# Float32 products for batches 0 and 1, and feed-forward weights taken unit by unit of both products

## The chip, the cores and the metric

The kernel runs on one core of one Trainium2 chip. Time is device microseconds of one execution. Before the change it is 1036.37 us, the median of three runs (1036.07 to 1036.69). The engines are TensorE (PE; its weight loads are shown as PEld), VectorE (DVE), ScalarE (ACT), GpSimd (POOL) and SyncE (SP), whose queue issues nearly all DMAs, the transposing ones too.

## The reference

Eight batches of eight heads, 576 tokens, 64 values a head. An attention with 32 memory slots is followed by a Fourier mix over tokens and channels and a feed-forward block of 512 to 2048 to 512:

```python
a = softmax(phi, over tokens)                  # 576 x 32 for each head
k_m, v_m = a.T @ k, a.T @ v                    # 32 x 64 each
x = softmax(q @ k_m.T / 8, over slots) @ v_m
u = x + real(fft(fft(x, tokens), channels))
ch = relu(layernorm(u) @ w_ch1) @ w_ch2
out = u + ch
```

All arrays are float32 and the result must be near float32.

## The kernel before

**Numbers.** To be near float32, most products are made of float16 halves: an operand is scaled, rounded to float16 (the high half), and the rest is rounded again (the low half); three products (high by high, low by high, high by low) are added in PSUM. Making halves takes a pass of ACT and a pass of DVE, or of ACT twice and POOL.

**Weights.** They arrive as 64-bit words (the host hands them over unchanged), 1 MB for each of NW = 8 units of `w1` and 8 of `w2`. `load_stage` (L710) brings a unit into a staging area; `to_f32` (L717) makes float32 of it: an Abs on ACT (L724), a shift and two combining passes on DVE (L726, L727, L737; for the units in `LP` the last is L732 on DVE and L735 on POOL), a sum of squares on ACT (L746) and a small product on PE (L220), from which `norm_scale` (L228, L236, L239) takes a power of two. `split_w1` (L752) and `prepare_w2` (L788) then write the float16 halves over the same memory.

**A batch** is the generator `background` (L810), which yields between steps. `pooling_weights` (L288) transposes phi on PE, takes the softmax over tokens, makes halves in `elt` and brings them back to token order in `et` by a transposing DMA (L319, helper L244). `pair_memory` (L323), for each of four pairs of heads, finds scales (L331 to L343), makes halves of k and v (L345 to L352) and multiplies by `et` in 30 float16 products of 64 columns (tile `pm`). `pair_scores` (L391) makes halves of q (L397, L398), 18 products (`psc`), the softmax over slots (L412 to L427) and sums and differences of tokens (L434 to L451). `values` (L465), `spectrum` (L500), `mix_m` (L547), `mix_x` (L532) and `add_mix` (L579) then make the rows of `u`: a batch has three groups of rows, t = 0, 1 and 2; group 2 is half a tile and shares its tile with the next batch's.

**Feed-forward.** The rows go in 18 chunks of two tiles of 128. `norm_chunk` (L612) normalises a chunk; for chunk 0 it transposes on PE and keeps float32, for the others it makes halves and uses a transposing DMA (`unring<-ud`). Chunk 0 goes through `ffn1_direct` (L634) and `ffn2_direct` (L649) in float32, the others through `ffn1` (L662, tile `ph`) and `ffn2` (L686, tile `po`), with relu and halves on ACT and DVE (L680, L681).

**Order.** The code's order is: batch 0 to its first two tiles; chunk 0 normalised; a loop over the 8 units of `w1`, each converted, used for chunk 0 and split, with the rest of batch 0 inside (`MB`, `M1`); a loop over the 8 units of `w2` that loads and converts them, with `norm_chunk(1)` inside (`N1`); then `advance(0)` (L887), which takes batch 1 as far as the ring of eight `u` tiles lets it (L890); then the main loop (L922), which for chunk 0 runs `ffn2_direct`, and beside it `ffn1` of the chunk after, and one step of a batch for each unit. Chunk 2 needs rows of batch 1. From this a planner, which simulates the engines, makes each engine's queue: it may take an instruction earlier than the code has it when its operands and memory are free in the simulation, and `tc.issue_after` forbids that for single instructions. On the chip each queue runs in its order, so an instruction that waits holds all behind it on its engine.

**Memory.** Staging areas of the weights (`W1_STAGE`, `W2_STAGE`, L705) lie in parts of `w2s` that are not yet in use and in the three areas of `stg`; `stg` is also where odd pairs of heads land (L277) and, from batch 1 on, where halves of k, v and q lie (L188 to L197).

Of the kernel before, what the change touches and what calls it, by code (L numbers as in the profile page):

```python
# [40 lines left out]
MB = 5  # L41
M1 = 2
N1 = 4
D2 = 8
# [10 lines left out]
W1_STAGE = [14, "0", "1", "2", 14, "0", "1", "2"]  # L55
W2_STAGE = [10, 14, "0", "1", 14, "0", "1", "0"]
# [75 lines left out]
def kernel(  # L132
# [50 lines left out]
    nc.gpsimd.memset(elt[:, :, S:], 0.0)  # L183
# [4 lines left out]
    def halves_area(b):  # L188

        if b == 0:  # L190
            v = hring[:, NHS:].rearrange("p a l b c -> p (a l b c)")
            t = w1t[:, NW].rearrange("p l k c -> p (l k c)")
        else:
            v = stg[:, 2]
            t = v[:, 4 * NST * P :]
        v = v[:, : 4 * NST * P].rearrange("p (l t w c) -> p l t w c", l=2, t=NST, w=2)
        return v, t[:, : 2 * NQ].rearrange("p (l c) -> p l c", l=2)  # L197
# [74 lines left out]
    def load_pair(b, g):  # L272
        r = rawt
        if b == 0 and g > 0:
            r = w2s.rearrange("p a l c -> p (a l c)").bitcast(F32)[:, RKQ * (g - 1) : RKQ * g]
        elif g % 2 == 1:
            r = stg[:, 0].bitcast(F32)  # L277
        nc.sync.dma_start(out=r[:, :KV], in_=raw[b, g, :, :KV])
        marks["q"] = nc.sync.dma_start(out=r[:, KV:], in_=raw[b, g, :, KVP:])
        return r  # L280
# [7 lines left out]
    def pooling_weights(b):  # L288
# [24 lines left out]
        for g in range(2):  # L313
            r = su[:, 2 + g : 3 + g]
            nc.scalar.activation(elt[:, 0, :S], pht[:, g], AF.Copy, scale=r)
# [7 lines left out]
    def pair_memory(b, g, r, vmf, ivs):  # L323
# [4 lines left out]
        kvs, _ = halves_area(b)  # L328
        am = tiny("am", 3, 1)
        for w in range(2):  # L330
            nc.scalar.activation(  # L331
                kvs[:, 0, :, w, :].bitcast(BF16), kv[:, :, w, :], AF.Square, accum_out=am[:, 1 + w : 2 + w]
            )
        nc.scalar.activation(
            kvs[:, 1, 0:3].rearrange("p t w c -> p (t w c)").bitcast(BF16), q, AF.Square, accum_out=am[:, 0:1]
# [8 lines left out]
        for w in range(2):  # L344
            nc.scalar.activation(kvs[:, 0, :, w, :], kv[:, :, w, :], AF.Copy, scale=sc[:, 1 + w : 2 + w])  # L345
            if w in KP:
                nc.scalar.activation(kv[:, :, w, :], kv[:, :, w, :], AF.Copy, scale=sc[:, 1 + w : 2 + w])  # L347
                nc.gpsimd.tensor_tensor(  # L348
                    out=kvs[:, 1, :, w, :], in0=kv[:, :, w, :], in1=kvs[:, 0, :, w, :], op=ALU.subtract
                )  # L350
            else:
                nc.vector.scalar_tensor_tensor(  # L352
                    out=kvs[:, 1, :, w, :],
                    in0=kv[:, :, w, :],
                    scalar=sc[:, 1 + w : 2 + w],
                    in1=kvs[:, 0, :, w, :],
# [3 lines left out]
        for w in range(2):  # L360
            i = 0
            for ka, kb in ((0, 0), (1, 0), (0, 1)):
                for t in range(NST):
                    mm(
                        pm[:, w * 64 : w * 64 + 64],
                        lhsT=kvs[:, ka, t, w, :],
# [24 lines left out]
    def pair_scores(b, g, q, sc, km, es, aeo):  # L391
# [4 lines left out]
        _, qs = halves_area(b)  # L396
        nc.scalar.activation(qs[:, 0], q, AF.Copy, scale=sc[:, 0:1])  # L397
        nc.vector.scalar_tensor_tensor(  # L398
            out=qs[:, 1], in0=q, scalar=sc[:, 0:1], in1=qs[:, 0], op0=ALU.mult, op1=ALU.subtract
        )  # L400
        for t in range(6):
            for i, (qa, ka) in enumerate(((0, 0), (1, 0), (0, 1))):
                mm(
                    psc[:, t * 64 : t * 64 + 64],
                    lhsT=qs[:, qa, t * P : (t + 1) * P],
# [21 lines left out]
        nc.gpsimd.tensor_tensor(out=a, in0=a, in1=sm.unsqueeze(2).to_broadcast([P, 12, M]), op=ALU.mult)  # L427
# [8 lines left out]
        for i, op in ((12, ALU.add), (16, ALU.subtract)):  # L436
            nc.gpsimd.tensor_tensor(out=a2[:, i : i + 4], in0=a[:, 0:4], in1=a[:, 4:8], op=op)  # L437
# [8 lines left out]
        nc.scalar.copy(out=aeo[:, 0, :, gs], in_=eov)  # L446
# [4 lines left out]
        nc.vector.scalar_tensor_tensor(  # L451
# [10 lines left out]
    def pair_transpose(b, g, ahl, attnT):  # L462
        transpose(attnT[:, g], ahl.rearrange("p t c -> p (t c)"), False, f"attnT_{b}_{g}")

    def values(b, vmf, ivs):  # L465
# [4 lines left out]
        nc.vector.tensor_reduce(out=isg, in_=ivs, axis=AX.X, op=ALU.max)  # L470
        nc.vector.reciprocal(out=sg, in_=isg)
# [8 lines left out]
        transpose(vbdt, vms.rearrange("p l g u c -> p (l g u c)"), False, f"vbd_{b}")  # L480
        vt = vts[min(b, 1)]
# [163 lines left out]

    def h_f32(j):
        return hring[:, j].rearrange("p l f c -> p (l f c)").bitcast(F32).rearrange("p (f t c) -> p f t c", f=UB, t=CH)
# [14 lines left out]
    def ffn1(c, unT, j, hs):  # L662
# [15 lines left out]
        h = hring[:, (c * NW + j) % NHS]  # L678
# [26 lines left out]
    def stage_area(i):  # L705
        if isinstance(i, str):
            return [stg[:, int(i)].bitcast(I32)]
        return [w2s[:, i : i + 2 * UB].rearrange("p a l c -> p (a l c)").bitcast(I32)]
# [8 lines left out]
    def to_f32(stages, dst, key):  # L717
# [28 lines left out]
        marks["sq" + key] = nc.scalar.activation(stages[0].bitcast(BF16)[:, :UW], dst, AF.Square, accum_out=sq[:, 0:1])  # L746
# [18 lines left out]
    def prepare_w1(j):  # L765

        t = w1_f32(j)
        if j not in parts_w1:
            parts_w1[j] = load_stage(w1[j], stage_area(W1_STAGE[j]))
        top = to_f32(parts_w1[j], t, f"1_{j}")  # L770
        s = s1[:, j : j + 1]
        norm_scale(s, is1[:, j : j + 1], top, 1, 9, f"w1_{j}")
# [4 lines left out]
    def stage_w2(j):  # L777
        top = to_f32(load_stage(w2[j], stage_area(W2_STAGE[j])), w2_f32(j), f"2_{j}")
# [31 lines left out]
    def background():  # L810
# [3 lines left out]
        for b in range(B):  # L814
# [6 lines left out]
            yield nt, 0  # L821
            for step in range(NG + 2):
                if step < NG and b == 0:
                    mem[step] = pair_memory(b, step, first[step], vmf, ivs)
                    yield nt, 0
                elif step < NG:
                    r = load_pair(b, step)
                if step >= 2:
# [9 lines left out]
            at = spectrum(b, aeo)  # L838
            full = slice(0, P)
# [164 lines left out]
```

## Time and profile before

| | |
|---|---|
| median of three runs | 1036.37 us |
| the profiled execution | 1033.89 us |
| its span, first to last instruction | 1032.1 us |
| mean granted TensorE clock | 0.977 |
| PE busy | 934.4 us, 91% |
| DVE busy | 592.0 us, 57% |
| ACT busy | 496.4 us, 48% |
| POOL busy | 240.8 us, 23% |

A busy PE is a PE with a product in flight; the ends of products are modelled, so the starts tell the rate. A row of the table by stage gives the stretch, its length, then for each engine the busy time and in brackets the number of instructions, then the granted clock of TensorE, the mean busy share of the DMA engines and GB/s. A row of the groups gives line, engine, operation, output and inputs, shapes and count, then busy time in all and the mean of one in ns, then the idle time ahead of them. A row of the chain of waits gives the start, the duration and what was running or waited for; the chain is followed backwards from the last instruction, so what is not in it could have been later.

### The profile page before, as it was taken

How to read it: one execution, taken by the hardware profiler on the slowest of the kernel's cores; microseconds unless marked ns; L12 is line 12 of the kernel's file. 1: busy time of each engine (PE TensorE's matmuls, PEld its weight loads, DVE VectorE, ACT ScalarE, POOL GpSimd, SP SyncE). 2: the span in 40 equal slices, each digit the busy share in tenths (PEclk: the TensorE clock that was granted, in tenths of full speed). 3: DMA queues.
4: the chain of work that ended last, by engine and by line, in shares of the span. 5: the costliest groups of instructions: out<-in, count | busy, mean ns of one | idle time of the engine just before them, and what ended most of it. 6: DMA issues, size and time to landing. Idle time of an engine off the chain costs nothing.

```text
span 1032.1 us, 19009 instructions
## 1 busy us (share of the span) xinstructions
PE 934.4 (91%) x7736; PEld 662.1 (64%) x7736; DVE 592.0 (57%) x1331; ACT 496.4 (48%) x986; POOL 240.8 (23%) x268
## 2 busy tenths in 40 slices
PE   1245999954999999999999999999999999999998
PEld 0224767634777677777676777777776777766664
DVE  5885966775676676557752467656745575311111
ACT  6563857655663655466541346365534553411110
POOL 1142432432331232233211013132221231300000
PEclk9996999976999999999999999999999999999999
DMA  9930454332531553154401173136312521201000
GB/s 357 308 71 19 195 180 113 74 105 44 138 95 38 101 121 87 39 113 119 85 28 41 18 163 96 38 55 162 92 48 37 120 15 38 41 21 35 8 22 20
DMA packets 124662, 90.30 MB, mean 87 GB/s; under 512 B 109344, under 2 KB 109344, under 8 KB 122272
## 3 DMA queue, kind: packets, MB, share of 16 engines
q1 hardware_dynamic: 124576, 89.10, 33.9%
q8 instruction: 60, 0.98, 0.4%
q14 instruction: 26, 0.21, 0.1%
HBM read 58.15 MB, written 9.44 MB: 65 GB/s over the span
## 4 chain that ended last, share of the span: by engine, by line
PE 85%; DVE 5%; DMA 3%; ACT 2%; POOL 2%; issue 1%; SPq 1%; DVEq 0%; POOLq 0%
PE ph L261 34%; PE po L690 33%; PE pp_t L261 3%; PE pm L261 3%; PE ph L641 3%; PE po L654 3%; PE psc L261 1%; PE px_t L261 1%; DMA w2s<-in_raw 1%; PE pa L514 1%; PE pv L487 1%; DMA et<-elt 1%; DMA unring<-ud 1%; DVE uring L583 1%; POOL ud L628 1%
## 5 line engine op out<-in xcount | busy, mean ns | idle before, releaser
L261 PE MATMUL ph<-unring,w1t 128*128 128x256 f16 x3264 | 392.1, 273 | 12.4 <-DMA unring<-ud 12.4
L690 PE MATMUL po<-w2s,hring 128*128 128x512 f16 x1632 | 378.0, 379 | 0.0
L261 PEld LDWEIGHTS <-w1t 128*128 128x128 f16 x3336 | 320.8, 99 | 79.5 <-DVE scratch L603 12.5
L690 PEld LDWEIGHTS <-hring 128*128 128x128 f16 x1632 | 157.6, 98 | 158.8
L681 DVE SCALAR_TENSOR_TENSOR hring<-ph,hring 128x512 f16<-128x512 f32 x136 | 93.3, 686 | 165.5 <-ACT hring L680 165.1
L680 ACT ACTIVATE hring<-ph 128x512 f16<-128x512 f32 x136 | 80.2, 590 | 168.9 <-PE ph L261 168.7
L427 POOL TENSOR_TENSOR aring<-aring,scratch 128x384 f32<-128x384 f32 x30 | 25.0, 834 | 178.5 <-DVE scratch L426 163.8
L261 PEld LDWEIGHTS <-stg 128*128 128x128 f16 x1344 | 54.1, 99 | 15.7 <-issue 3.6
L607 POOL TENSOR_TENSOR scratch<-scratch,small 128x1 f32<-128x1 f32 x36 | 21.9, 612 | 153.2 <-DVE scratch L606 143.1
L348 POOL TENSOR_TENSOR stg<-rawt,stg 128x640 f16<-128x640 f32 x14 | 20.5, 1461 | 135.2 <-ACT rawt L347 125.2
L628 POOL TENSOR_TENSOR ud<-un,ud 128x1024 f16<-128x1024 f32 x17 | 36.2, 2129 | 46.7 <-ACT ud L627 46.7
L261 PE MATMUL pp_t<-vh,at 128*128 128x255 f16 (+3 forms) x288 | 41.1, 291 | 1.7 <-ACT at L529 1.5
L261 PE MATMUL pm<-et,hring 128*128 128x64 f16 x120 | 8.2, 241 | 35.7 <-DMA et<-elt 18.6
L569 DVE SCALAR_TENSOR_TENSOR share<-pp_t,scratch,small 128x257 f32<-128x257 f32 (+1 forms) x48 | 21.1, 481 | 32.5 <-ACT small L566 32.3
L422 ACT ACTIVATE aring<-aring,scratch 128x384 f32<-128x384 f32 x30 | 18.2, 608 | 43.0 <-DVE aring L421 43.0
L261 PE MATMUL pm<-et,stg 128*128 128x64 f16 x840 | 34.9, 194 | 4.4 <-POOL stg L348 2.7
L446 ACT CAST aeo<-eo 128x384 f16<-128x384 f32 x30 | 15.3, 510 | 45.2 <-DVE eo L443 45.1
L261 PEld LDWEIGHTS <-at 128*128 128x128 f16 (+1 forms) x288 | 30.0, 109 | 8.2 <-ACT at L529 1.8
L583 DVE SCALAR_TENSOR_TENSOR uring<-px_t,scratch,share 128x256 f32<-128x256 f32 (+1 forms) x80 | 33.9, 476 | 0.2
L627 ACT CAST ud<-un 128x1024 f16<-128x1024 f32 x17 | 17.8, 1045 | 33.4 <-DVE un L608 25.1
L412 DVE TENSOR_REDUCE scratch<-psc 128x12 f32<-128x384 f32 x32 | 17.8, 555 | 27.9 <-PE psc L261 27.8
L437 POOL TENSOR_TENSOR aring<-aring 128x128 f32<-128x128 f32 x60 | 33.2, 574 | 2.3
(199 smaller groups left out, 1318.6 us busy)
## 6 DMA issues: line engine op xcount, KB each, us to landing
stg<-in_w SPq DMA_DIRECT2D x11, 1024.0 KB, 8.5
rawt<-in_raw SPq DMA_DIRECT2D x15, 640.0 KB, 4.5
out<-uring SPq DMA_DIRECT2D x36, 256.0 KB, 2.1
stg<-in_raw SPq DMA_DIRECT2D x14, 640.0 KB, 4.8
rawt<-in_raw SPq DMA_DIRECT2D x15, 384.0 KB, 3.3
stg<-in_raw SPq DMA_DIRECT2D x14, 384.0 KB, 3.1
phs<-in_raw SPq DMA_DIRECT2D x32, 160.0 KB, 3.9
w2s<-in_w SPq DMA_DIRECT2D x5, 1024.0 KB, 6.4
```

Source lines behind the costliest of these rows:

```text
L261: m = nc.tensor.matmul(out, lhsT=lhsT, rhs=rhs, start=start, stop=stop)
L427: nc.gpsimd.tensor_tensor(out=a, in0=a, in1=sm.unsqueeze(2).to_broadcast([P, 12, M]), op=ALU.mult)
L437: nc.gpsimd.tensor_tensor(out=a2[:, i : i + 4], in0=a[:, 0:4], in1=a[:, 4:8], op=op)
L569: nc.vector.scalar_tensor_tensor(out=tm[rows, w * NJ : (w + 1) * NJ], in0=pp[rows, :NJ], scalar=beta[rows], in1=qs[rows], op0=ALU.mult, op ...
L583: nc.vector.scalar_tensor_tensor(out=u[rows, hs], in0=px[rows, hs], scalar=igx[rows], in1=tm[rows, w * NJ + half : w * NJ + half + 256], o ...
L607: nc.gpsimd.tensor_tensor(out=rs, in0=rs, in1=half, op=ALU.pow)
L628: marks[f"ul{c}"] = nc.gpsimd.tensor_tensor(out=ud[:, 1], in0=un, in1=ud[:, 0], op=ALU.subtract)
L641: nc.tensor.matmul(ph, lhsT=w[:, k, f * P : (f + 1) * P], rhs=unTs[0][:, k], start=(k == 0), stop=(k == NK - 1))
L654: nc.tensor.matmul(po[t], lhsT=h[:, f, t], rhs=w[:, f], start=(j == 0 and f == 0), stop=(j == NW - 1 and f == UB - 1),)
L680: nc.scalar.activation(h[:, 0], phv, AF.Relu)
L681: nc.vector.scalar_tensor_tensor(out=h[:, 1], in0=phv, scalar=0.0, in1=h[:, 0], op0=ALU.max, op1=ALU.subtract)
L690: nc.tensor.matmul(po[t], lhsT=hs[j][:, lh, f * 2 + t], rhs=w2s[:, j * UB + f, lw, :], start=(j == 0 and f == 0 and i == 0), stop=(j == NW ...
```

## The change

- Batches 0 and 1 (`b < NX`) keep the pooling weights in float32 (`et32`, in the memory of `et`), transposed on PE; `pair_memory` makes ten float32 products of k and v as they come, and `pair_scores` six float32 products of q. The scales and halves of k, v, q and km are left out for these batches; `values` finds its scale from a sum of squares.
- For batch 0 the transposes of the attention weights and of the values are made on PE and copied by ACT, and three steps of `pair_scores` go from POOL to DVE.
- In batch 0 all four `pair_memory` come ahead of the scores in the code. The loads of its pairs are tied to one another in order and the weights' loads come behind them, three units of both products at once.
- One loop over the units: load, convert `w1`, `ffn1_direct`, convert `w2`, `ffn2_direct`, split `w1`, two steps of the batches. The conversions but the first of `w1` may not start ahead of chunk 0's normalisation (`GATE1`, `GATE2`: on DVE not ahead of the mark `un1`, L608; on ACT not ahead of `uh0`, L624).
- Staging areas: parts of `w1t`, of `w2s`, `stg` 1 and 2, and once the end of `hring` with two tiles of `uring`. Batch 1's pairs use `rawt` and `stg` 0. The sum of squares writes its unused output to `elt`.
- Chunk 0 is finished ahead of the main loop, which starts at chunk 1; four units of chunk 1's `ffn1` are in the code ahead of `norm_chunk(2)`.

```diff
+STEPS = 2
+NX = 2
+GATE1 = [[]] + [["un1", "uh0"]] * 7
+GATE2 = [["un1", "uh0"]] * 8
-W1_STAGE = [14, "0", "1", "2", 14, "0", "1", "2"]
-W2_STAGE = [10, 14, "0", "1", 14, "0", "1", "0"]
+W1_STAGE = ["w4", "w6", "s1", "w6", "s1", "s2", "s1", "x"]
+W2_STAGE = ["b10", "b14", "s2", "b10", "b14", "x", "s2", "s1"]
...
-    nc.gpsimd.memset(elt[:, :, S:], 0.0)
+    nc.gpsimd.memset(et.rearrange("p g l t c -> p (g l t c)"), 0.0)
...
@@ in load_pair @@
+        for part, src in ((r[:, :KV], raw[b, g, :, :KV]), (r[:, KV:], raw[b, g, :, KVP:])):
+            with tc.issue_after(marks["q"].ins) if b == 0 and "q" in marks else nullcontext():
+                marks["q"] = nc.sync.dma_start(out=part, in_=src)
...
@@ in pooling_weights @@
+            if b < NX:
+                nc.scalar.activation(pht[:, g], pht[:, g], AF.Copy, scale=r)
+                pt = psg.tile([P, 512], F32, tag="g", name=f"pt_e{b}_{g}")
+                for t in range(4):
+                    nc.tensor.transpose(pt[:, t * P : (t + 1) * P], pht[:, g, t * P : (t + 1) * P], identf)
+                nc.vector.tensor_copy(out=et32[:, g, :4], in_=pt.rearrange("p (t c) -> p t c", c=P))
+                half_t = pl[0 : S - 4 * P, (2 + g) * P : (3 + g) * P]
+                nc.tensor.transpose(half_t, pht[:, g, 4 * P :], identf)
+                nc.scalar.copy(out=et32[0 : S - 4 * P, g, 4], in_=half_t)
+                continue
...
@@ in pair_memory @@
+        if b < NX:
+            pm = psg.tile([P, 512], F32, tag="g", name=f"pm_{n}")
+            mm = groups()
+            for w in range(2):
+                for t in range(NST):
+                    mm(
+                        pm[:, w * 64 : w * 64 + 64],
+                        lhsT=kv[:, t, w, :],
+                        rhs=et32[:, g // 2, t, 64 * (g % 2) : 64 * (g % 2) + 64],
+                        start=(t == 0),
+                        stop=(t == NST - 1),
+                    )
+            kmf = share[:, g * 64 : g * 64 + 64] if b == 0 else tiny("kmf", 64, 2)
+            nc.vector.tensor_tensor(out=kmf, in0=pm[:, 0:64], in1=mk[:, 0:64], op=ALU.mult)
+            nc.vector.tensor_tensor(
+                out=vmf[:, g],
+                in0=pm[:, 64:128].unsqueeze(1).to_broadcast([P, 2, 64]),
+                in1=mk[:, 0:64].unsqueeze(1).to_broadcast([P, 2, 64]),
+                op=ALU.mult,
+            )
+            return q, None, kmf, 1.0 / 8.0
...
@@ in pair_scores @@
+        if b < NX:
+            for t in range(6):
+                mm(psc[:, t * 64 : t * 64 + 64], lhsT=q[:, t * P : (t + 1) * P], rhs=km, start=True, stop=True)
...
+        eng = nc.gpsimd if b else nc.vector
+        eng.tensor_tensor(out=a, in0=a, in1=sm.unsqueeze(2).to_broadcast([P, 12, M]), op=ALU.mult)
...
-            nc.gpsimd.tensor_tensor(out=a2[:, i : i + 4], in0=a[:, 0:4], in1=a[:, 4:8], op=op)
+            eng.tensor_tensor(out=a2[:, i : i + 4], in0=a[:, 0:4], in1=a[:, 4:8], op=op)
...
-        transpose(attnT[:, g], ahl.rearrange("p t c -> p (t c)"), False, f"attnT_{b}_{g}")
+        transpose(attnT[:, g], ahl.rearrange("p t c -> p (t c)"), b == 0, f"attnT_{b}_{g}")
...
@@ in stage_area @@
+        if name[0] == "s":
+            return [stg[:, i].bitcast(I32)]
+        if name[0] == "w":
+            return [w1t[:, i : i + 2].rearrange("p a l k c -> p (a l k c)").bitcast(I32)]
+        if name[0] == "b":
+            return [w2s[:, i : i + 2 * UB].rearrange("p a l c -> p (a l c)").bitcast(I32)]
+        return [
+            hring[:, 6:8].rearrange("p a l f c -> p (a l f c)").bitcast(I32),
+            uring[:, 5:7].rearrange("p a c -> p (a c)").bitcast(I32),
+        ]
...
+    for j in range(3):
+        load_weights(j)
...
     for j in range(NW):
-        prepare_w1(j)
-        if j == M1:
-            while made < MB:
-                made, room = next(bg)
+        if j not in parts_w1:
+            load_weights(j)
+        after(GATE1[j], prepare_w1, j)
         ffn1_direct(j)
+        after(GATE2[j], stage_w2, j)
+        ffn2_direct(j, po)
         split_w1(j)
-    for j in range(NW):
-        after([f"2_{j - D2}"] if j >= D2 else gate, stage_w2, j)
-        if j == N1:
+        advance(0, steps=STEPS)
+        if made >= 2 * CH and 1 not in unTs:
             unTs[1] = norm_chunk(1)
+    nc.gpsimd.memset(elt[:, :, S:], 0.0)
     scale_w2()
+    finish(0, po)
     vts.append(load_vt())
+    prepare_w2()
...
-    advance(0)
-    for n in range(n_steps):
+    run_ffn1(NW + 4)
+    advance(CH, CH * 3)
+    unTs[2] = norm_chunk(2)
+    for n in range(NW, n_steps):
...
-        run_ffn1(n + NHS)
+        run_ffn1(n + 4 if n + 4 <= 2 * NW else n + NHS)
```

`load_weights(n)` issues the loads of unit n of `w1` and of `w2`, each into its staging area and each behind the one before.

More of the change, by code (lines that the diff above doesn't have):

```diff
@@ L186 @@
     hring = const.tile([P, NW, 2, 4, P], F16, name="hring")
[L188 to L197, printed above, removed]
+    nk = 2 * NST * P
+    kvs = [stg[:, 2, i * nk : (i + 1) * nk].rearrange("p (t w c) -> p t w c", t=NST, w=2) for i in range(2)]
+    qs = [stg[:, 2, 2 * nk + i * NQ : 2 * nk + (i + 1) * NQ] for i in range(2)]
+    et32 = et.rearrange("p g l t c -> p (g l t c)").bitcast(F32).rearrange("p (g t c) -> p g t c", g=2, t=NST)
     nc.gpsimd.memset(half, -0.5)
@@ L445, in pair_scores @@
         eov = eo.rearrange("p e t c -> p (e t) c")
-        nc.scalar.copy(out=aeo[:, 0, :, gs], in_=eov)
+        marks[f"a{b}_{g}"] = nc.scalar.copy(out=aeo[:, 0, :, gs], in_=eov)
         av4 = aeo.rearrange("p l (e t) c -> p l e t c", e=2)
@@ L703, in finish, with stage_area @@
             nc.sync.dma_start(out=out[idx], in_=u)
[L705 to L708, printed above, removed]
+    def stage_area(name):
+        i = int(name[1:] or 0)
+        if name[0] == "s":
[8 more added lines that the diff above has]
+        ]
     def load_stage(src, stages):
@@ L821, in background @@
             yield nt, 0
+            if b == 0:
+                for g in range(NG):
+                    mem[g] = pair_memory(b, g, first[g], vmf, ivs)
             for step in range(NG + 2):
[L823 to L826, printed above, removed]
+                if step < NG and b > 0:
                     r = load_pair(b, step)
-                if step >= 2:
+                if step >= 2 and b > 0:
                     pair_transpose(b, step - 2, ahl.pop(step - 2), attnT)
@@ L870, with load_weights @@
     marks["load"] = marks["q"]
-    parts_w1 = {0: load_stage(w1[0], stage_area(W1_STAGE[0]))}
     with tc.issue_after(marks["load"].ins):
         vts = [load_vt()]
-        nc.sync.dma_start(out=ct, in_=ct_d)
+        marks["load"] = nc.sync.dma_start(out=ct, in_=ct_d)
+    parts_w1, parts_w2 = {}, {}
+    def load_weights(n):
+        for parts, w, stages in ((parts_w1, w1, W1_STAGE), (parts_w2, w2, W2_STAGE)):
+            parts[n] = load_stage(w[n], stage_area(stages[n]))
+    for j in range(3):
+        load_weights(j)
     bg = background()
```

80 lines of the change are left out of this document (38 added, 42 removed).

## The prediction

> **What bounds the kernel now.** I read the page's head first, then the table by stage, then the chain of waits.
>
> ```profile
> span 1032.1 us, 19009 instructions
> PE 934.4 (91%) x7736; PEld 662.1 (64%) x7736; DVE 592.0 (57%) x1331; ACT 496.4 (48%) x986; POOL 240.8 (23%) x268
> PE   1245999954999999999999999999999999999998
> ```
>
> PE is busy for 934 of 1032 us, and the slices say where the other 98 us lie: in the first four slices and in the ninth to eleventh. The stages are cut at the events that end them.
>
> ```profile
> 0.00:100.48 100.48, 32.01 (x303) 24.92 (x304) 71.79 (x147) 53.48 (x98) 24.35 (x39) 0.92 0.57 191
> 100.48:160.00 59.52, 59.52 (x259) 41.90 (x258) 46.39 (x101) 42.80 (x69) 21.68 (x10) 0.99 0.48 168
> 160.00:209.30 49.30, 49.30 (x426) 33.64 (x425) 33.66 (x61) 35.00 (x64) 17.47 (x16) 1.00 0.47 109
> 209.30:255.40 46.10, 21.15 (x199) 15.73 (x198) 31.27 (x84) 25.39 (x57) 11.21 (x14) 0.70 0.24 60
> 500.00:900.00 400.00, 400.00 (x3449) 284.51 (x3447) 228.84 (x531) 188.55 (x393) 93.05 (x107) 1.00 0.31 68
> ```
>
> The front, up to chunk 0's first float32 product at 100.5, leaves PE idle for 100.5 - 32.0 = 68.5 us. The direct products (to 160) and chunk 1 (to 209.3) fill PE. Then PE waits 25 us, 46.1 - 21.2, for the rows of batch 1. From 255.4 on PE is full, and the change leaves that part's work alone. So **the time is set by when chunk 2 starts: 255.4**, and each microsecond by which it starts earlier is one off the end.
>
> ```profile
> 6.93 15.02 DMA w2s<-in_raw
> 22.04 9.89 DMA et<-elt
> 251.01 4.27 DMA unring<-ud
> 255.41 6.11 PE ph L261 x41
> ```
>
> In the front the chain stands first on a load of batch 0's pairs, 15 us, behind four loads of weights, and then on a transposing DMA, 9.9 us. After that it is mostly DVE.
>
> **The front.** What DVE does there for the weights is one row, its instructions on `w1t` up to 100.48; behind it the same row for L352 and for L398, to 255.4, and groups of what else goes:
>
> ```profile
> 0.00:100.48 100.48, 30.92 (x28) 0.92 0.57 191
> 0.00:255.40 255.40, 7.92 (x9) 0.91 0.47 146
> 0.00:255.40 255.40, 12.15 (x9) 0.91 0.47 146
> L384 DVE TENSOR_TENSOR scratch<-scratch 128x64 f16<-128x64 f32 x8 | 2.6, 328 | 4.1 <-ACT scratch L383 4.1
> L316 DVE SCALAR_TENSOR_TENSOR elt<-phs,scratch,elt 128x576 f16<-128x576 f32 x5 | 4.1, 819 | 5.1 <-ACT elt L315 5.0
> L236 DVE TENSOR_SCALAR scratch<-scratch 128x3 f32<-128x3 f32 x9 | 2.0, 220 | 0.1
> L298 DVE TENSOR_REDUCE scratch<-pf 128x1 f32<-128x512 f32 x6 | 4.1, 684 | 6.4 <-PE pf L297 6.4
> L421 DVE TENSOR_TENSOR aring<-psc,scratch 128x384 f32<-128x384 f32 x6 | 3.3, 550 | 0.0
> ```
>
> All of the `w1` conversion (24 instructions) is now inside the front, with four halves of q: 30.9 of DVE's 71.8 us. For batch 0 there also go four L352 (7.92 / 9 = 0.88 each, 3.5 us), two L316 (1.6), four L384 (1.3) and some 25 instructions on scales, at most 0.22 each, say 5.5. That leaves 71.8 - 30.9 - 3.5 - 1.6 - 1.3 - 5.5 = 29. Added: two copies of `et32` like L298 (1.4), and per pair what comes over from POOL, one like L421 (0.55) and two like the L439 below (0.29), together 4.5. The first `w1` unit's conversion stays, 0.7 + 1.2 + 1.2 and three scales, 3.6. Sum 38.5 us.
>
> ```profile
> 0.00:25.00 25.00, 3.19 (x12) 2.36 (x12) 13.77 (x24) 14.93 (x27) 3.91 (x14) 1.00 0.93 354
> 50.00:75.00 25.00, 10.45 (x118) 7.28 (x119) 21.72 (x50) 15.40 (x29) 14.01 (x17) 1.00 0.30 64
> 8.23 0.17 DVE L302 TENSOR_SCALAR scratch<-scratch 128x2 f32<-128x2 f32 x1
> 9.96 0.67 ACT L306 ACTIVATE phs<-pf,scratch 128x512 f32<-128x512 f32 x1
> 11.77 0.20 ACT L307 ACTIVATION_READ_ACCUMULATOR phs<-pl,scratch 128x1 f32 x1
> 37.37 0.55 DVE L412 TENSOR_REDUCE scratch<-psc 128x12 f32<-128x384 f32 x1
> 83.03 0.86 DVE L451 SCALAR_TENSOR_TENSOR aeo<-aeo,small,eo 128x128 f16<-128x128 f16 x1 [0.58 <-ACT aeo L446]
> 97.27 0.59 ACT L624 COPY unring<-pt_unT 128x512 f32<-128x512 f32 x1 [0.21 <-PE pt_unT L623]
> ```
>
> Batch 0's four pairs with phi are 4.85 MB; at 354 GB/s and with the queue's first 3 us the last lands at 16.7, not 22. The exponentials can start when the maxima are done (L302, 8.4). They take 2.0 us (9.96 to 11.97); the sums, the scaling, five transposes, a copy like L298 (0.7), ten products and six are an estimate of 6.5 us more (4 to 8), so the first scores reach DVE (L412) at about 17 instead of 37.4. From there to the last pair's L451 DVE has 38.5 less 4 already done and 6.5 that lie behind, 28 us of work; at the 87% at which it ran from 50 to 75 that is 32 us, to 49. From that L451 to the end of the last copy to `unring` it is now 97.9 - 83.0 = 14.8 us, kept. **Chunk 0's first product: about 64** (bounds 56 and 72: PE may take all four `pm` ahead of the first `psc`, 5 us; DVE may fill 95%). PE's added work there hides in its idle time: 10 float32 transposes, 28 float16 ones; ACT's six or so copies go beside DVE's chain, 3 us if they don't. The larger memset on POOL is over long before POOL's first other work.
>
> ```profile
> 187.70 2.12 POOL L796 TENSOR_TENSOR w2s<-w2s 128x1024 f16<-128x1024 f32 x1
> 187.92 2.05 DVE L439 TENSOR_TENSOR eo<-aring 128x128 f32<-128x128 f32 x1
> 218.70 0.29 DVE L439 TENSOR_TENSOR eo<-aring 128x128 f32<-128x128 f32 x1 [0.36 <-POOL aring L437]
> ```
>
> The same DVE instruction takes 0.29 us alone and 2.05 beside a POOL instruction that it cannot pass. The Trainium skill, "SBUF — State Buffer", section "Who interferes with whom", says that a VectorE instruction with two inputs in SBUF and a GpSimd instruction that reads SBUF lock one another out for the whole instruction. By that rule taking work off POOL would free DVE as well, and the front's sum would be about 6 us less; the trace agrees on this pair of rows, but two POOL instructions per pair remain, so I leave the sum as it is.
>
> **The loop over units.** Everything that is moved behind the normalisation is paid here. DVE's work up to 255.4 is now 71.8 + 46.4 + 33.7 + 31.3 = 183 us. Less, for both batches: eight of nine L352 (7.0) and of nine L398 (10.8), L384 (2.6), four L316 (3.3), scales (7); in all 31. More: four copies, two norms and the steps from POOL, 8. So 160 us. Behind the loop lie parts that stay with chunk 1:
>
> ```profile
> L681 DVE SCALAR_TENSOR_TENSOR hring<-ph,hring 128x512 f16<-128x512 f32 x8 | 5.5, 687 | 2.6 <-ACT hring L680 2.6
> L798 DVE SCALAR_TENSOR_TENSOR w2s<-w2s,small 128x1024 f16<-128x1024 f32 x5 | 6.4, 1279 | 0.4 <-ACT w2s L793 0.4
> L583 DVE SCALAR_TENSOR_TENSOR uring<-px_t,scratch,share 128x256 f32<-128x256 f32 (+1 forms) x20 | 8.4, 476 | 0.0
> 113.05 1.73 PE ph L641 x8
> 121.59 3.54 PE po L654 x8
> 344.79 2.62 PE ph L261 x24
> ```
>
> 5.5 for relu, 6.4 for `w2`, four outputs of 0.7, batch 1's mixes (ten L583 and six like it, 7.3), and some 7 for chunk 2's norm and batch 2's first steps: 29. The loop then holds 160 - 38.5 - 29 = 92.5 us of DVE. PE has there 128 direct products at 1.73 / 8 and 64 at 3.54 / 8, 56 us, with the rest of batches 0 and 1 some 87: the 130 that PE did from 100.5 to 255.4, plus 6, less chunk 1's 49. ACT has less than DVE. So DVE sets the loop: 92.5 / 0.87 = 106 us and the last unit's `ffn2_direct`, 3.5: 110. Bounds 87 (PE alone) and 130 (below). What is queued behind the two gates on DVE and ACT is only conversions, which nobody needs sooner.
>
> Float32 products of 64 columns are not in the trace. Eight L641 of 256 columns start every 0.216 us, 24 float16 ones every 0.109, so float32 costs two, where three halves cost three; ten for thirty is at worst even. The Trainium skill, "FP8 and Floating Point Precision", section "TensorE Precision Notes", has true float32 at four passes through the array; by it ten would cost forty, and PE some 4 us more, in a loop that DVE sets. The rows disagree with it, so the sum goes by two.
>
> **The sum.** 64 + 110 = 174; chunk 1 then fills PE for 49.3 as it does now, with its first `ffn1` covering the split of `w2`, and chunk 2's rows are ready under it: 223.5, 32 earlier than 255.4. The span becomes 1000, the profiled execution's 1033.89 becomes 1002, and the median, 2.5 above that execution, 1036.4 - 32 = **1004**.
>
> **The rivals.** *DVE fills better.* With fewer instructions on POOL and a deep backlog DVE runs at 95% and loses 6 us of lock in the front and 6 in the loop: 57 + 95 + 49 = 201, a gain of 54, **982**. For it: the 0.29 row; against: 87% is the best long stretch seen.
>
> ```profile
> 152.41 0.28 PE pf L297 x2
> ```
>
> *Batch 1's chain holds PE.* From its first transposes, at 152.4, to chunk 2's transposing DMA at 251.0 batch 1 now takes 99 us, though DVE is only 70% busy over the last two stages; PE takes its queue in order, and direct products stand behind batch 1's. If the loop takes 130, chunk 2 starts at 243: **1023**. Against: the steps are spread two to a unit.
>
> *Slower: the reloading of the staging areas.* Ten of the sixteen units can be loaded only when an earlier unit has been converted out of their area; on SP's queue such a load, tied in order, holds all behind it, batch 1's pairs and the transposing DMAs too.
>
> ```profile
> stg<-in_w SPq DMA_DIRECT2D x11, 1024.0 KB, 8.5
> ```
>
> If each of the last five rounds stands 8.5 us bare, the loop is 42 us longer: **1046**. It decides from 32 / 5 = 6.4 us a round. Against: areas come free a whole unit ahead, some 13 us of DVE work.
>
> *Nothing moves*: the planner spends the front's gain waiting for batch 1 after chunk 1 as now, 1036.
>
> **How the numbers follow.** The forecast has 0.57, better filling 0.18, batch 1's chain 0.15, reloading 0.08, nothing 0.02. A measurement can tell about 0.2%, 2 us, from no change. Faster 0.57 + 0.18 + 0.15 = 0.90, same 0.02, slower 0.08. The range runs from the well-filled case, 980, past the chain's case to 1030; the bounds of the front (8 us either way) are inside it.
>
> **What would show it.** Right: the first L641 at 56 to 72; no weights on DVE ahead of it but one unit; DVE over 85% busy in the loop and PE at about 80%; chunk 1's first float16 `ph` near 174 and chunk 2's near 224 with no idle PE in between. Wrong: PE idle between chunk 1 and 2; PE full in the loop (then the gain is larger); waits of ACT at L724 for `in_w` of several us a unit; a first L641 past 75.

## The result, and the profile after

| | before | after |
|---|---|---|
| median | 1036.23 us (1036.07 to 1036.69, 4 runs) | 1003.35 us (996.36 to 1005.71, 4 runs) |
| profiled execution | 1033.89 us, span 1032.1 | 996.36 us, span 994.6 |

The ratio is 0.9678, with a 95% interval of 0.9633 to 0.9723. A second measurement gave 1003.42 us beside 1035.95, 0.969 (0.9673 to 0.9707). The forecast was 1004. These four executions of the kernel before lie within 0.6 us of one another, and those beside the later runs within 2.3 to 4.4. The changed one spreads over 9: of nine executions one, the profiled, took 996.4 us and the others 1002.5 to 1005.9. The last experiments are about that.

The page's head and PE's slices after:

```profile
span 994.6 us, 18655 instructions
PE 948.0 (95%) x7644; PEld 675.4 (68%) x7644; DVE 566.9 (57%) x1287; ACT 456.2 (46%) x913; POOL 225.7 (23%) x249
PE   5679899789999999999999999999999999999998
```

PE's idle time fell from 1032.1 - 934.4 = 97.7 us to 994.6 - 948.0 = 46.6, and its busy time rose by 13.6: 51.1 - 13.6 = 37.5 us of span. PE's first four slices read 1, 2, 4 and 5 before and 5, 6, 7 and 9 now; the ninth and tenth read 5 and 4 before and 8 and 9 now. (The eleventh, which the prediction counts among the idle ones, was full.) The table by stage (the stretch, its length, busy time of PE, PEld, DVE, ACT and POOL with the number of instructions, granted clock, DMA share, GB/s), cut at the first direct product, at the end of the direct products, at the start of the wait for `w2` and at chunk 2:

```profile
0.00:59.49 59.49, 32.95 (x257) 28.59 (x257) 36.01 (x100) 22.24 (x47) 11.78 (x23) 0.88 0.71 260
59.49:139.20 79.71, 74.84 (x328) 52.28 (x329) 68.24 (x113) 45.14 (x77) 21.54 (x11) 0.94 0.53 182
139.20:177.00 37.80, 36.23 (x349) 32.10 (x347) 28.12 (x88) 25.59 (x51) 16.20 (x20) 1.00 0.40 106
177.00:209.40 32.40, 24.67 (x169) 14.58 (x168) 24.80 (x58) 25.04 (x51) 10.31 (x8) 0.84 0.44 98
209.40:500.00 290.60, 288.62 (x2558) 205.49 (x2557) 182.45 (x421) 152.11 (x311) 80.06 (x91) 1.00 0.33 80
```

The first direct product comes at 59.5 where it came at 100.5, and the direct products take 79.7 us. Behind them PE is not yet free: from 139.2 to 177 lies batch 1's chain, which the planner moved out of the loop, with chunk 1's `ffn1` under it, and from 177 to 209.4 chunk 1's `ffn2` waits for the halves of `w2`, with PE idle for 7.7 us, some 4.8 of them for these halves. From 209.4 on PE is as full as before. The waits of PE, longest first, and the chain of waits where `w2` gets its scale:

```profile
PE pt_e L314 <- ACT phs L311: 6.0, 1, 6.0
PE pt_unT L657 <- DVE un L642: 5.3, 1, 5.3
...
PE po L728 <- ACT w2s L838: 3.3, 2, 2.3
PE ph L675 <- DVE w1t L784: 2.8, 1, 2.8
```

```profile
175.81 0.16 DVE small L827
177.60 0.06 DVE small L828
179.32 0.06 DVE small L829
180.94 0.07 DVE small L830
182.44 0.14 DVE small L831
184.29 1.18 DVE w2s L843
```

The first of five small steps on the scale (L827) starts at 175.8, and each of the others comes 1.5 to 1.8 us behind the one before, because DVE and ACT take the mixes of batch 1 between them.

### The profile page after: what moved, and what is told of

It reads as the page before. It is cut to its first block, busy times and chain, and to the rows that moved or that the text cites. A ratio compares the mean times of both kernels' runs of the same rounds, so it can differ in the third digit from the quotient of the medians.

```text
span 994.6 us, 18655 instructions
## 1 busy us (share of the span) xinstructions
PE 948.0 (95%) x7644; PEld 675.4 (68%) x7644; DVE 566.9 (57%) x1287; ACT 456.2 (46%) x913; POOL 225.7 (23%) x249
## 4 chain that ended last, share of the span: by engine, by line
PE 83%; DVE 9%; ACT 4%; issue 2%; DMA 1%; POOL 1%; SPq 0%; DVEq 0%; ACTq 0%; POOLq 0%
PE po L728 34%; PE ph L255 34%; PE pm L255 4%; PE pp_t L255 3%; PE psc L255 2%; PE po L692 1%; PE px_t L255 1%; PE ph L675 1%; PE pa L548 1%; PE pv L521 1%; DVE uring L617 1%; DVE un L642 1%; DVE w1t L784 1%; DVE w2s L774 1%; DMA rawt<-in_raw 1%
## 5 line engine op out<-in xcount | busy, mean ns | idle before, releaser
L255 PEld LDWEIGHTS <-w1t 128*128 128x128 f16 x3264 | 316.7, 98 | 66.7 <-issue 3.0
L641 POOL TENSOR_TENSOR scratch<-scratch,small 128x1 f32<-128x1 f32 x36 | 24.3, 690 | 165.7 <-DVE scratch L640 153.7
L255 PEld LDWEIGHTS <-stg 128*128 128x128 f16 x1152 | 45.4, 98 | 8.1 <-ACT stg L370 1.6
L662 POOL TENSOR_TENSOR ud<-un,ud 128x1024 f16<-128x1024 f32 x17 | 36.3, 2135 | 47.4 <-ACT ud L661 47.4
L373 POOL TENSOR_TENSOR stg<-rawt,stg 128x640 f16<-128x640 f32 x12 | 17.3, 1438 | 127.0 <-ACT rawt L372 107.1
L255 PE MATMUL pm<-et,stg 128*128 128x64 f16 (+1 forms) x780 | 36.6, 199 | 2.0 <-ACT stg L370 1.4
L440 DVE TENSOR_REDUCE scratch<-psc 128x12 f32<-128x384 f32 x32 | 17.7, 554 | 36.4 <-PE psc L255 36.3
L675 PE MATMUL ph<-unring,w1t 128*128 128x256 f32 x128 | 34.4, 417 | 3.2 <-DVE w1t L784 2.8
L255 PE MATMUL pp_t<-vh,at 128*128 128x255 f16 (+3 forms) x288 | 36.7, 274 | 0.3 <-ACT at L563 0.2
L675 PEld LDWEIGHTS ph<-unring,w1t 128*128 128x128 f32 x128 | 26.3, 209 | 11.9 <-issue 4.3
L450 ACT ACTIVATE aring<-aring,scratch 128x384 f32<-128x384 f32 x24 | 14.6, 608 | 42.2 <-DVE aring L449 42.2
L692 PE MATMUL po<-w2s,hring 128*128 128x512 f32 x64 | 31.3, 618 | 2.1 <-ACT hring L678 2.1
```

Of the source, the lines that this page charges most:

```text
L255: m = nc.tensor.matmul(out, lhsT=lhsT, rhs=rhs, start=start, stop=stop)
L641: nc.gpsimd.tensor_tensor(out=rs, in0=rs, in1=half, op=ALU.pow)
L662: marks[f"ul{c}"] = nc.gpsimd.tensor_tensor(out=ud[:, 1], in0=un, in1=ud[:, 0], op=ALU.subtract)
L675: nc.tensor.matmul(ph, lhsT=w[:, k, f * P : (f + 1) * P], rhs=unTs[0][:, k], start=(k == 0), stop=(k == NK - 1))
L692: nc.tensor.matmul(po[t], lhsT=h[:, f, t], rhs=w[:, f], start=(j == 0 and f == 0), stop=(j == NW - 1 and f == UB - 1),)
```

## Experiments

Two theories stood against each other at first: that the gain comes from the float32 products of batches 0 and 1, which take a third of batch 0's work off DVE, or that it comes from what the diff gives most lines to, the joint loop with its gates and staging areas.

**Float32 alone, in the kernel before.**

```diff
+NX = 2
@@ in pooling_weights, pair_memory, pair_scores, values @@
+        if b < NX:
...
```

> The kernel before with float32 products for batches 0 and 1 and nothing else of the change (weights staged, converted and ordered as before, transposes of attention weights and values by DMA, the three steps on POOL). Theory (most of the gain is the halves and transposing DMAs that batches 0 and 1 lose): some 19 us of DVE and a 10 us DMA wait leave the front, first direct product at 78 to 84 us instead of 100.5, PE's wait ahead of chunk 2 about 10 us instead of 25, time about 1010 (1000 to 1020). Rival (the order of the conversions is what counts): first product at 95 or later, time 1028 or more.

999.41 us (997.32 to 1000.05), ratio 0.9642 (0.9628 to 0.9656). Its stages, up to the first direct product, to the end of the direct products, and the stretch ahead of chunk 2:

```profile
0.00:77.94 77.94, 39.95 (x244) 34.47 (x245) 57.19 (x116) 32.81 (x58) 23.08 (x36) 0.72 0.69 237
77.94:151.50 73.56, 69.97 (x314) 48.33 (x314) 52.36 (x102) 46.41 (x76) 24.38 (x11) 0.97 0.39 136
...
202.00:219.15 17.15, 12.71 (x112) 9.57 (x112) 13.16 (x44) 9.76 (x27) 4.40 (x5) 0.98 0.21 48
```

A gain as large as the whole change's is here, in a few lines: 36.6 us, where the change gives 32.9. The front is 22.5 us shorter than before's, though all of `w1` is still converted in it, and the stall of 25 us ahead of chunk 2 has become one of 4.4. The time is 10 us less than I had expected. So the rest of the change, taken together, is worth about nothing: 3.9 us less than nothing by the medians, and 1.0 us more by the two profiled executions (997.3 and 996.4), which both had PE's full clock in batch 0's products or most of them (see the spread below).

**The gate alone, and with float32.** In the kernel before, the conversions of `w1` but the first wait for chunk 0's normalisation:

```diff
-        prepare_w1(j)
+        after(gate if j else [], prepare_w1, j)
```

> The kernel before with only the gate: w1 units 1 to 7 may not be converted ahead of chunk 0's normalisation. Theory (DVE pays for the conversions wherever they stand): 22 us leave the front, first product at about 80 us, but the direct products then run at DVE's pace and end near 160 as now; time 1036, 1028 to 1044. Rival (the order is what counts): the front's gain stays, time 1020 or less.

> The kernel before with float32 products for batches 0 and 1 and the gate, without the joint loop and the new staging areas. Theory: first product at about 60 us, PE's wait ahead of chunk 2 stays in part because batch 1 still comes behind both loops; time about 1008 (1000 to 1016), near the changed kernel's 1003. Rival (the joint loop over both products is what counts): 1020 or more.

Alone it costs 10.6 us: 1046.58 us (1043.48 to 1047.6), ratio 1.0096 (1.0077 to 1.0114). With float32 it gives 1005.46 (1000.9 to 1006.26), 6 us more than float32 without it. First the gate alone, then both:

```profile
0.00:86.67 86.67, 30.43 (x288) 22.97 (x288) 47.07 (x117) 40.92 (x82) 22.27 (x39) 0.93 0.56 172
86.67:173.00 86.33, 76.00 (x355) 52.45 (x356) 75.75 (x135) 57.26 (x94) 28.06 (x10) 0.97 0.48 165
173.00:215.00 42.00, 38.31 (x337) 25.27 (x335) 28.79 (x53) 30.71 (x49) 14.80 (x12) 0.99 0.43 112
215.00:262.00 47.00, 21.44 (x206) 16.77 (x206) 31.96 (x84) 23.76 (x55) 15.24 (x19) 0.65 0.24 61
```

```profile
0.00:63.37 63.37, 34.14 (x228) 30.07 (x228) 35.35 (x86) 19.15 (x42) 18.23 (x36) 0.80 0.66 225
63.37:148.90 85.53, 77.98 (x354) 53.10 (x355) 73.41 (x130) 55.41 (x87) 27.71 (x10) 0.95 0.48 166
209.00:221.84 12.84, 2.67 (x35) 2.57 (x32) 9.67 (x32) 7.38 (x19) 3.22 (x3) 0.73 0.22 41
```

The gate does bring the first direct product forward, from 100.5 to 86.7 and from 77.9 to 63.4. It is paid back behind: the same conversions now stand in the loop (DVE 75.75 and 73.41 us there), batch 1 comes as late as before or later, and PE waits ahead of chunk 2, 25.6 us and 10.2. **An earlier first product is worth nothing by itself**; what counts is when the rows that chunk 2 needs are there.

**The changed kernel without its gates.**

```diff
-GATE1 = [[]] + [["un1", "uh0"]] * 7
-GATE2 = [["un1", "uh0"]] * 8
+GATE1 = [[]] * 8
+GATE2 = [[]] * 8
```

> The changed kernel without its two gates: conversions may start as soon as the weights are there. Theory: DVE idles 23 of the front's 59.5 us, so conversions mostly fill gaps; the first product comes 5 to 12 us later and the loop is shorter by about as much; time 1003 plus or minus 6. Rival (the gates hold the front short and the rest does not give it back): first product 15 to 25 us later, time 1015 or more.

1016.93 us (1016.8 to 1019.55), 13.6 more by the medians. At PE's full clock in batch 0's products, as both profiled executions had it for most of them, it is 20.5 more (1016.85 against 996.36). Up to the first direct product, then to the end of the direct products:

```profile
0.00:77.00 77.00, 29.01 (x192) 24.58 (x193) 56.98 (x107) 32.05 (x54) 19.70 (x23) 0.70 0.77 284
77.00:108.50 31.50, 12.40 (x88) 10.19 (x86) 28.03 (x48) 13.44 (x21) 7.81 (x4) 0.61 0.47 163
108.50:191.30 82.80, 82.80 (x447) 61.16 (x445) 39.31 (x125) 43.72 (x88) 22.57 (x27) 1.00 0.30 77
```

DVE's instructions on the weights ahead of the first direct product, those on `w1t` and then those on `w2s`:

```profile
0.00:108.50 108.50, 0.00 (x0) 0.10 (x1) 29.64 (x28) 13.60 (x16) 0.00 (x0) 0.67 0.68 249
0.00:108.50 108.50, 8.95 (x64) 8.60 (x64) 21.26 (x25) 12.53 (x15) 11.04 (x4) 0.67 0.68 249
```

That is 50.9 us of conversions, and the first direct product comes at 108.5. In this order of the loads the gates are needed; they repair what the early loads of both products would do.

**The batches' other edits, in the kernel before.** Float32, the chained loads, batch 0's transposes on PE and three steps from POOL to DVE, with the two old loops. One of the batches' edits is not in it, though its expectation speaks of every edit: the order in which all four `pair_memory` come ahead of the scores.

```diff
-        transpose(attnT[:, g], ahl.rearrange("p t c -> p (t c)"), False, f"attnT_{b}_{g}")
+        transpose(attnT[:, g], ahl.rearrange("p t c -> p (t c)"), b == 0, f"attnT_{b}_{g}")
...
```

> The kernel before with every edit for the batches and none of the weights' staging and loop: float32 for batches 0 and 1, batch 0's pairs loaded in a chain, its attention and value transposes on PE, three steps from POOL to DVE. The theory that the gain comes from shortening the batches' own chain: with float32 alone at 999, the first direct product at 77.9 and 17 us between chunks 1 and 2, the other edits bring the first direct product to 64 to 72, chunk 2 to 207 to 215, and the time to 988 to 996. The rival, that the conversions of the weights ahead of the direct products set that point: direct products not before 75, and the time stays at 997 to 1001.

> The changed kernel itself, beside the kernel before and the other three of this group. Expected 1003 (996 to 1006), as measured already; it tells whether the spread of 9 us between its own executions comes back.

1014.71 us (1014.54 to 1015.18), where the changed kernel beside it took 1003.42: 15 us slower than float32 alone, a miss in sign. The first direct product is at 93.1. The waits of PE ahead of it:

```profile
PE pt_attnT L255 <- POOL ud L475: 18.6, 3, 13.2
PE pt_attnT L255 <- POOL ahring L475: 6.9, 1, 6.9
```

PE takes its queue in order. A transpose that is moved from the DMA queue to PE waits there for its halves, made on POOL, and the next pair's products wait behind it, 25.5 us in all. The changed kernel has all pairs' products and scores ahead of the first such transpose, and no such wait. That this order alone makes up the 15 us was not tried, and the waits are not all of it. The profiled execution had PE at half its clock up to 76.7 us (see the spread below), and its chain of waits holds 40 products of `pm` and three times 12 of `psc` at 0.21 us each:

```profile
15.49 8.43 PE pm L264 x40
62.92 2.57 PE psc L264 x12
```

That is 8.43 + 3 x 2.57 = 16.1 us, of which the full clock would save about half. So up to 8 of the 15 us may be the clock.

**Is DVE or PE the bound of the loop?** PE was 94% busy there. This run takes one pass of the weights' conversion off DVE (and with it 9 us off POOL).

```diff
-            if key in LP:
+            if True:
+                pass
+            elif key in LP:
```

> The changed kernel, leaving out the pass that combines the low words in the conversion of the weights (16 passes on DVE of about 1.2 us, in part POOL's). The step of the prediction, that DVE sets the loop over units: 12 to 20 us less, 983 to 991. The rival, that PE is the bound there once batch 1 is pushed behind it (94% busy in the trace): 1 to 5 us less, 998 to 1002.

987.59 us (986.94 to 988.94) beside 1003.42, **15.8 us less, as DVE would have it**. The changed kernel in the profile of that group, its front, its loop and what follows; then loop and what follows without the pass:

```profile
0.00:68.05 68.05, 44.39 (x256) 40.59 (x256) 36.34 (x100) 22.29 (x47) 11.78 (x23) 0.96 0.62 227
68.05:147.33 79.28, 73.69 (x326) 51.66 (x327) 67.98 (x112) 44.83 (x77) 21.54 (x11) 0.95 0.53 183
147.33:300.00 152.67, 141.81 (x1229) 103.42 (x1228) 108.03 (x260) 93.84 (x183) 53.35 (x57) 0.97 0.34 86
```

```profile
67.61:148.53 80.92, 78.87 (x395) 58.36 (x396) 55.79 (x131) 53.92 (x95) 20.80 (x17) 0.97 0.61 203
148.53:300.00 151.47, 147.06 (x1287) 107.36 (x1286) 105.77 (x248) 93.27 (x184) 48.69 (x51) 1.00 0.32 74
```

The loop is no shorter, but 69 more of PE's products fit into it (395 for 326), and behind it PE idles for 4.4 us in place of 10.9. The gain shows behind the loop: chunk 2's first product comes at 195.8 us for 217.1, and from the loop's end to it there are 47.3 us for 69.7. So DVE's work does not set the length of the loop, but how much of PE's work is done when the loop ends, and through it when chunk 2 starts. An engine that gets more work whenever there is a gap looks full whatever sets the pace.

**The scale of `w2`.**

```diff
+        if key[0] == "2":
+            return None
...
+    nc.gpsimd.memset(is2, 2.0**-10)
```

> The changed kernel, leaving out the sums of squares of the units of w2 and with a fixed power of two in place of the scale worked out from them. The theory that PE's 7.7 idle us between 177 and 209 are the split of w2, begun late because the last unit's sum comes late: 5 to 9 us less, 994 to 998, and no wait for the split. The rival, that chunk 1's second product or batch 1's rows would wait at the same place for something else: less than 2 us.

996.29 us (991.5 to 1000.62), 7.1 less by the medians. But the median stands between two pairs, 991.5 and 992.2 (mean granted clock 0.983) and 1000.4 and 1000.6 (0.988). The changed kernel's execution of 996.4 has 0.983 too, and the four beside this run, 1002.5 to 1005.9, have 0.988 to 0.991. Like against like the sums cost 4 to 5 us in the one group and about 3 in the other, below the 5 to 9 that were expected; that the clock sorts them so is inferred, since only one execution of each kernel in this group has a trace. The wait for ACT at `w2s` is gone, though a wait of 8.0 us for POOL in the loop has come in its place in the profiled execution.

**The spread, and PE's rate.** In the execution of 996.4 us and in the one profiled with the last group, of 1005.9, the chain of waits has batch 0's products, 80 in each, as

```profile
16.36 9.59 PE pm L255 x80
25.95 1.35 PE psc L255 x12
...
124.79 2.18 PE pm L255 x20
```

```profile
16.01 16.96 PE pm L255 x80
32.97 5.13 PE psc L255 x24
```

0.12 us each in the first (the first eight at 0.21, the rest at 0.11), 0.21 in the second, the same instructions in the same order; the first direct product is at 59.5 and at 68.05. The column of the granted clock reads 0.88 in the front of the shorter execution and 0.96 in that of the longer one, but it can't be trusted here: the first record of the clock in the trace comes at 17.7 us in the one and at 52.0 in the other, both times to full, and the column counts the time ahead of it as full. At 17.7 us the products of the shorter execution go over to 0.11 us. To see whether the rate is set by what PE did just before, I put transposes of the identity, which nobody reads, into PE's idle time ahead of these products.

```diff
+        for i in range(30 if b == 0 else 0):
+            with tc.issue_after(last.ins):
+                last = nc.tensor.transpose(pl[:, 3 * P :], identf, identf)
```

> The changed kernel with 30 float32 transposes of the identity, of 128 columns and with an unused result, on PE between the transposes of phi and those of the exponentials, where PE has 6 us of nothing to do; every engine's order is otherwise the same but for one conversion on DVE. In the executions of the changed kernel shown so far batch 0's float32 products of 64 columns start either every 0.11 us (the execution of 996.4) or every 0.21 us from the first to the last (1005.9), at a granted clock that reads 1.00 in both. The theory that the array's own rate at that point makes the spread, and that dense work ahead of the products settles it: products every 0.11 us, first direct product at 59 to 60, 994 to 998 in all executions. The rival, that something else (a load that lands late) makes the spread: 1000 to 1006, or both.

1008.16 us (999.32 to 1009.79): no gain, and the spread stayed. The transposes went into a tile that DVE reads for the maxima, so the exponentials came 4.5 us later, and behind the transposes PE stood idle for 5.65 us. The profiled execution is the one of 999.3, with products every 0.12 us on average: it too starts them at 0.21 us behind the gap and goes over to 0.11 behind the fifth.

With 28 such transposes, the kernel before with float32, the batches' edits (again without the order of the pairs) and the gate:

> The kernel before with every edit for the batches, with the conversions of w1 held behind chunk 0's normalisation, and with 28 such transposes on PE; none of the joint loop, of the staging areas and of the order of the weights' loads. Beside the changed kernel with the transposes it tells what the joint loop is worth. The theory that it is worth nothing: within 4 us of that kernel, 992 to 1000. The rival, that it brings what was planned (chunk 0 done earlier, chunk 1 behind it without a stall): 1003 to 1010 here.

1016.83 us (1014.1 to 1019.78), 8.7 above the run before; the two intervals, 0.9787 to 0.9851 and 0.9671 to 0.9764, lie apart. So joint loop and order of the pairs together bring some 9 us back, of what the gate and the other edits cost; this kernel too waits on PE for POOL's halves, 10.8 us, so the loop's own share is not separated.

**One step of the batches to a unit** (`STEPS = 1`), with the 30 transposes still in:

> The changed kernel with the transposes and with one step of the batches to a unit in place of two, so that batch 1 stands still later in the code. The theory that the loop is short because batch 1 is out of it, and that the sums of squares of the last units, which stand on PE behind batch 1, delay the split of w2: the direct products end 3 to 8 us earlier, and 988 to 994. The rival, that chunk 2 then waits for batch 1's rows: 998 to 1008, with PE idle ahead of chunk 2.

994.92 us (994.67 to 995.95), 13.2 below the kernel with two steps. First two steps, then one, behind the direct products:

```profile
141.40:300.00 158.60, 145.63 (x1265) 106.19 (x1264) 110.89 (x267) 96.84 (x189) 53.96 (x58) 0.98 0.35 83
```

```profile
71.33:153.80 82.47, 77.24 (x339) 53.75 (x340) 72.73 (x130) 52.05 (x88) 23.34 (x13) 0.93 0.51 176
153.80:300.00 146.20, 144.01 (x1275) 106.97 (x1274) 104.83 (x234) 86.42 (x168) 48.05 (x53) 1.00 0.38 87
```

PE's idle time there falls from 13.0 us to 2.2. The expectation had the place wrong: the direct products end later, not earlier (153.8 for 141.4), after a front with products at 0.21 us (first direct product at 71.3 for 63.5). What is gone is the idle time behind them, the wait for `w2` included.

**The two together, with the transposes right up to the work.** 44 of them, into a tile that no engine reads before the exponentials are there.

```diff
-STEPS = 2
+STEPS = 1
...
+            warm = psg.tile([P, 512], F32, tag="g", name="pt_e0_0")
+            for i in range(44):
+                with tc.issue_after(last.ins):
+                    last = nc.tensor.transpose(warm[:, :P], identf, identf)
```

> One step of the batches to a unit, as in the run before, with 44 transposes of the identity in place of 30, written where no engine reads before the exponentials are there, so that they fill PE's idle time right up to the transposes of the exponentials and hold nothing up. The theory that dense work just ahead sets the array's rate, and that the 5.7 idle us behind the 30 lost it again: the products of 64 columns every 0.11 us throughout, the first direct product at 58 to 62 (71.3 there), 981 to 987, executions within 3 us of one another. The rival, that those products fall back to 0.21 us however PE comes to them: only the 4.5 us come back by which the 30 transposes held up the exponentials, the first direct product at 66 to 68, 989 to 992.

**984.17 us (982.61 to 985.3, 5 runs), ratio 0.9495 (0.9479 to 0.9511)**, 19 below the changed kernel. PE in the run before and in this one (start, duration, instruction; a row's duration is that of the group):

```profile
7.26 3.97 PE L296 MATMUL pl<-identf 128*128 128x128 f32 x30
16.88 1.11 PE L317 MATMUL pt_e<-identf,phs 128*128 128x128 f32 x4 [5.65 <-ACT phs L314]
...
19.07 4.37 PE L255 MATMUL pm<-et,rawt 128*128 128x64 f32 x20
```

```profile
7.39 6.25 PE L299 MATMUL pt_e<-identf 128*128 128x128 f32 x44
13.64 0.66 PE L320 MATMUL pt_e<-identf,phs 128*128 128x128 f32 x4
...
15.15 2.44 PE L255 MATMUL pm<-et,rawt 128*128 128x64 f32 x20
```

In the run before PE reached its full rate in the 30 transposes (the first six start every 0.21 us, the others every 0.11), lost it in 5.65 idle us and did not get it back through 80 products at 0.21 us. Here four transposes of the exponentials take 0.66 us for 1.11, and the products start every 0.11 us from the first to the last. In these two executions the records of the clock begin ahead of the products, at 8.3 and 10.0 us, so that its column (third from the end) can be read. The rows are from just ahead of the first of batch 0's products to the last, in the run before and in this one:

```profile
19.00:46.00 27.00, 27.00 (x129) 27.00 (x128) 11.85 (x31) 4.61 (x9) 1.37 (x2) 0.50 0.92 338
```

```profile
15.00:30.00 15.00, 14.61 (x129) 14.37 (x128) 7.59 (x19) 3.15 (x6) 0.00 (x0) 1.00 1.02 417
```

So the two rates are the granted clock, half and full. The first direct product is at 61.1, inside what was expected, and five executions lie within 2.7 us, with a mean clock of 0.981 to 0.986. The theory holds, and the rival falls.

## Why the prediction came out right

*Front.* 64 was forecast, with bounds of 56 and 72; it is 59.5 in the execution above and 68.05 in the one with products every 0.21 us. DVE has 36.0 us there (38.5 forecast), and only one unit of the weights ahead of the first tokens. PE took all four `pm` ahead of the first scores, the bound that I had named at 5 us. That PE itself could run at half its clock there was in no term.

*Loop.* **This is the step that was mis-sized: 110 us forecast, 79.7 measured.** DVE is 68.24 / 79.71 = 86% busy, the fill that I took, but it has 68 us of work there and not 92.5, because the planner put most of batch 1 behind the direct products. In turn chunk 1 is not 49.3 us of full PE: from 139.2 to 209.4 there are 70 us, with PE idle for 9.3. The two errors largely cancel, since both were shares of one sum: I had 160 us of DVE's work ahead of chunk 2, and up to 209.4 it has 36.01 + 68.24 + 28.12 + 24.80 = 157.2. That DVE's work sets when chunk 2 starts is borne out by the run without the low words (21.3 us earlier there, 15.8 us off the median); that it sets the loop's own length is not, since that loop stayed as long. A PE full in the loop and a PE idle ahead of chunk 2 stood among my signs that the step was wrong, and both came.

*Sum.* "Each microsecond by which it starts earlier is one off the end" does not hold as it stands: chunk 2 starts 255.4 - 209.4 = 46.0 us earlier in the execution of 996.4, and the span ends 37.5 earlier. Chunk 2's start is not the same point in the two kernels. Before, all 96 products of chunk 1's `ffn2` were done by then; in the changed kernel 50 are. The other 46, every 0.216 us, come behind it, less 48 short products of batch 2 that come ahead (1.4 us): 8.5 us. Where all 96 come ahead, as with float32 alone, the rule holds: 36.3 us at chunk 2, 36.7 at the end. So in before's terms chunk 2 starts at 217.9; 223.5 was forecast (the terms add up to 223.3). The execution of 1005.9 ends 1032.1 - 1004.1 = 28 us earlier. For a profiled execution 1002 was forecast; the latter is longer by 4 us, which its front has. That the median meets 1004 within 1 us is luck in part: a front that was 4.5 us shorter than forecast at the full clock, a loop 30 shorter, a chunk 1 that took 21 more and left 8.5 behind, and the half clock, which adds some 7 us to most executions.

*Gates.* I had costed them at nothing, since only conversions stand behind them. That does not hold for the order of the work: they are worth 13.6 us by the medians in this order of the loads and cost 10.6 in the old one.

*Float32 of 64 columns.* "At worst even" was wrong. A row of before's chain has thirty float16 products; ten float32 ones take half of the 2.18 above, 1.09, and where they start every 0.21 us, 2.1:

```profile
171.20 0.88 PE pm L261 x30
```

PE paid for that and the step still won, because PE had the time and DVE had not. The rule of the Trainium skill, "FP8 and Floating Point Precision", section "TensorE Precision Notes", which has true float32 at four passes, has forty passes in place of thirty, 1.17 us as an estimate, near the 1.09; the 0.216 us of 256 columns still stand for two. In the last run the float32 transposes of 128 columns start every 0.11 us, as these products of 64 do; what sets the 0.11 us at 64 columns is not shown.

*Rivals.* Batch 1's chain did hold PE, but behind the loop and not in it: 13 us, which the run with one step takes away. Reloading of the staging areas shows no wait of note; a load of a unit into `stg` takes 5.0 us and is hidden. DVE's fill stayed at 86%, so nothing came of 95%.

## What to carry to other kernels

Count the work of the engine that sets the end over the whole stretch to the next fixed point, not stage by stage: moving it between stages, with gates or a joint loop, gave or cost some 10 us here, depending on what else was moved, and taking it away, with float32 in place of halves, gave 36.6. A point in time that two kernels share by name, such as the start of a chunk, measures the gain only if the same work lies ahead of it in both. A diff with many parts should be priced one part at a time, since the few lines of float32 alone gave as much as all of it, and `STEPS` (13.2 us) was worth more than the loop that it belongs to (some 9, with the order of the pairs). Before work is moved onto an engine that takes its queue in order, ask what will stand behind it there.

## What the runs showed of the hardware

Float32 products of 64 columns start every 0.11 us at best, and float32 transposes of 128 columns do the same (four take 0.66 us in the last run, with the last one's end in it): 64 columns gained nothing over 128 here.

The same products go every 0.11 or every 0.21 us, as the granted clock is full or half (0.50 and 1.00 in the rows of the last two runs). In these traces the clock is missing up to its first change (at 8.3 to 76.7 us of the span), and a mean that counts the missing time as full hides the half rate: 0.96 for the front of the execution of 1005.9 us. The starts of like products show it.

What PE did in the microseconds before decides in part. Behind dense transposes right up to the products all of them went at full rate, in the one execution that has a trace. In the two runs with 30 transposes 5.65 idle us took the rate away. Behind a gap it came back with the ninth product in the execution of 996.4 us, and only at 52.0 us in the one of 1005.9. The Trainium skill, "TensorE: Matmul & The Clock Gate", section "Part 1: The HAM clock gate", has the array at half its clock until some 3.4 us of sustained work, and the return to half after an idle stretch of that length. The loss in 5.65 idle us agrees. The first half does not hold for these products: in the run with one step PE is busy with them for 27 us without a gap, and the clock stays at 0.50. Nor do they always keep a full clock: with float32 alone it falls to half at 27.3 us, among the last pair's products. That they keep the array itself busy for only half of the time, as a transpose of twice the columns goes in the same time, may be why; no run here shows it.
